# A scan and a mixture of adapters on one core: stores of four chunks in 8 KB rows, x stepped over four chunks, and new orders kept as lists

## The chip, the cores and the metric

The kernel runs on one core of one Trainium2 chip. The metric is the device time of one execution in microseconds (us): median 202.64 of three runs of the kernel before (202.54 to 202.82).

## The reference

Two steps, one after the other. The first is a linear recurrence over time for 8 sequences of 6400 steps and 128 channels; the second treats its 51,200 results as tokens x, finds 8 logits for each, keeps the two largest, and adds to each token the output of the two adapters chosen (rank 16), weighted by a softmax of the two logits.

```python
h = np.zeros((B, D))
for t in range(S):
    h = a[:, t] * h + b[:, t]
    out[:, t] = h
x = out.reshape(B * S, D)
logits = x @ w_gate
topk = np.argpartition(-logits, K, axis=1)[:, :K]          # K = 2
...
for e in range(E):
    ...
    z = x[mask] @ A[e]
    delta[mask] += w[mask, k, None] * (z @ B[e])
return x + delta
```

a and b are 26.2 MB each, the result is 26.2 MB, all float32.

## The kernel before, in words

The tokens are cut into 100 chunks of 512 rows (`C`), four blocks of 128 (`J`). Everything about a chunk carries its number. These are the steps, with the names that the order uses.

- **Loads** `la`, `lb` (L707): a and b, two chunks at a time (512 KB), into one of 6 places (`NL`). A partition holds eight consecutive rows, 4 KB. The first four chunks come singly, in rows of 2 KB.
- **Transposes** `A`, `B`, `P` (L728): PE turns a and b into PSUM (`pA`, `pB`), so that channels are partitions and time runs along the row. `P` does b of one chunk and a of the next together, in 64 x 64 pieces.
- **`ae`** (L746): ACT copies a out of PSUM.
- **Scan** `sc` (L784): DVE's tensor_tensor_scan over 512 steps; its result, in f16, is x transposed, in one of `NX = 24` places `xT`. Scan c needs scan c-1.
- **`Z`, `ze`** (L804, L810): units of six blocks (four at both ends). A block of x is the weight, the router and the eight A matrices side by side are streamed (136 columns); ACT copies the result to `zl`, with room for `NZ = 120` blocks.
- **Gating** (L841 to L880), in groups of up to 24 blocks: `g1` to `g8`, `w1`. Maximum, difference, mask, second maximum, and so on; steps 2, 3, 5, 6 and 7 are on DVE or on POOL (`q`), `w1` is ACT's sigmoid.
- **`mu`** (L913 POOL, L917 DVE): z times the weights. **`T`** (L926): PE turns the product. **`te`** (L932 ACT, L935 DVE): copies it out of PSUM. **`D`** (L940, L941): for each block two matmuls into one bank, x itself (x as the weight, times the identity) and the adapters' output. **`oe`** (L955 ACT, L952 DVE): copies the sum to `outt`, with room for `NO = 72` blocks.
- **Stores** `st` (L986): two chunks at a time, four singles at the end.

A block of x takes every fourth column of a chunk, since a partition of the output holds four consecutive rows (`xblock`, in the function `bass_associative_scan_2x2__then__mixture_of_adapters_kernel`):

```python
def xblock(b):
    return xcols(b // J).rearrange("d (p j) -> d j p", j=J)[:, b % J, :]
...
dst = out[r0 : r0 + m * C, :].rearrange("(h p j) d -> p h j d", p=128, j=J)
view = outt[:, q : q + m * J, :].rearrange("p (h j) d -> p h j d", j=J)
```

So a store of two chunks writes 256 rows of 2 KB. Each engine works through its own list of operations and waits in it for what the next one needs: an operation that has to wait holds all behind it on its engine. SP's list holds loads and stores together. The lists come out of `Program.schedule`: each operation has a rank (a base that grows with its chunk, plus an entry of the table `NUDGE`), and the operations of an engine go out by rank. Which engine does an operation is set by lists of numbers: `TE_ACT` (40 of the 100 `te` go to ACT), `OE_DVE` (7 `oe` to DVE), `MU_DVE` (12 `mu` to DVE), `GATE_DVE` (20 gating steps to DVE). `SPLIT` cuts the store that begins with chunk 68 into 124 and 4 partitions. The ranks give, for the end of SP's list:

```
... la96 st60 lb96 la98 st62 lb98 st64 st66 st68 st70 st72 st74 st76 st78 st80 st82 st84 st86 st90 st88 st92 st94 st98 st97 st99 st96
```

and for PE around the 48th chunk and after the last front transposes:

```
... P47 T31 D30 Z31 D31 T32 P48 D32 Z32 T33 P49 D33 T34 P50 Z33 D34 ...
... B99 T85 T84 Z66 D85 D84 Z67 T87 Z68 T86 D87 T91 D86 T89 T90 D91 T88 D89 D90 D88 T95 T92 T94 T93 D95 D92 D93 D94 T97 T98 D97 D98 T99 T96 D99 D96
```

Of the kernel before, what the change touches and what calls it, by code (L numbers as in the profile page):

```python
# [10 lines left out]
PERIOD = 6  # L11
FREE = {"pe": 0.0, "act": 0.105, "dve": 0.082, "pool": 0.044, "sp": 0.0}
SEEN = {"pe": 0.06, "act": 0.04, "dve": 0.055, "pool": 0.08, "sp": 0.0}
SELF = {"pe": 0.0, "act": 0.035, "dve": 0.035, "pool": 0.078, "sp": 0.0}
PE_WAIT = 0.08
PE_FREE = 0.1
SP_MARGIN = 2.0
LAND_MARGIN = 1.0
Q_RATE = {3: 4.2e-3, 5: 2.1e-3, 7: 2.1e-3}
SCAN_SELF = 0.13  # L20
ISSUE = {"sp": 0.52, "act": 0.45}
LOAD_RATE = 387e3
STORE_RATE = 413e3
DMA_START = 0.3
DMA_SEEN = 1.15
DMA_DEPTH = 9
FIRST_ISSUE = 0.7
FIRST_WORK = 0.73
TABLES = 1.32
NUDGE = {  # L30
# [182 lines left out]
}  # L213
WINDOW = {'pe': 0.0, 'act': 0.0, 'dve': 0.0, 'pool': 0.0, 'sp': 0.0}
START = (-999, "", 0)
FIRST = -9999
EARLY = -400
LEAD = [1, 2]
# [4 lines left out]
FLAT = []  # L223
FILL = {}
# [70 lines left out]
class Program:  # L295
# [5 lines left out]
    def __init__(self):  # L301
        self.ops = []
# [802 lines left out]
```

## Time and profile before

| | |
|---|---|
| median of three runs | 202.64 us |
| profiled execution, first to last instruction | 200.9 us |
| bytes read, written | 52.56 MB, 26.21 MB |
| first scan starts | 6.18 us |
| last load issued by SP | 162.58 us |
| DVE, ACT, PE, POOL busy | 176.2, 175.8, 177.7, 136.9 us |

The profile shows one execution. A group of instructions is named by line, engine, operation and tiles, as out<-in (partitions x elements, type); behind it stand its count, its busy time, the mean of one in ns, and the idle time of the engine just before them with what ended it. PEld is the loading of a matmul's weights, which runs beside PE. SPq is SP's queue of DMA instructions. PE's busy time counts the whole passage of a matmul through the array, so a busy PE isn't PE at its peak.

### The profile page before, as it was taken

The page shows a single profiled execution, that of the slowest core. Times are in us where ns is not written, and L with a number is a line of the kernel's source. Part 1 is how long each engine was busy: PE and PEld are TensorE (multiplying, and loading weights), DVE is VectorE, ACT ScalarE, POOL GpSimd, SP SyncE. Part 2 cuts the span into 40 slices and gives each one's busy share as a digit, 9 for nine tenths or more (in the row PEclk, how much of TensorE's full clock was granted, in tenths as well). Part 3 has the DMA queues.
Part 4 walks back from the last instruction along what each step waited for, and adds up shares of the span by engine and source line. Part 5 has one row for each costly group of instructions (what it writes and reads, how often), then busy time and mean ns, then how long its engine had stood idle before and what let it go on. Part 6 is the DMA issues. An engine that isn't in the chain of part 4 may idle for free.

```text
span 200.9 us, 7611 instructions
## 1 busy us (share of the span) xinstructions
PE 177.7 (88%) x3192; PEld 155.9 (78%) x3192; DVE 176.2 (88%) x283; ACT 175.8 (88%) x327; POOL 136.9 (68%) x176
## 2 busy tenths in 40 slices
PE   6888978999899969999988999899999997898970
PEld 6766867888688858888878888787888886787860
DVE  1699999999999968999897999798899998999971
ACT  2589998999779969999997999899999998899970
POOL 1331559498989887797987797868876466767420
PEclk9999999999999999999999999999999999999998
DMA  6999999999999999999999999999999999999985
GB/s 216 378 412 408 411 405 401 411 406 404 414 409 400 412 416 409 401 417 407 409 413 409 410 409 412 413 410 411 417 408 410 414 410 409 406 381 387 357 338 215
DMA packets 29065, 79.26 MB, mean 395 GB/s; under 512 B 2664, under 2 KB 2920, under 8 KB 29032
## 3 DMA queue, kind: packets, MB, share of 16 engines
q1 hardware_dynamic: 28456, 78.39, 99.0%
q8 instruction: 25, 0.41, 0.8%
q10 hardware_dynamic: 576, 0.40, 0.7%
q14 instruction: 8, 0.07, 0.1%
HBM read 52.56 MB, written 26.21 MB: 392 GB/s over the span
## 4 chain that ended last, share of the span: by engine, by line
DMA 33%; PE 27%; DVE 16%; ACT 15%; SPq 5%; issue 2%; DVEq 0%; ACTq 0%
DMA a_tm<-in_a_dram 26%; DVE xT L784 9%; DMA out_dram<-outt 7%; ACT zl L810 5%; PE pZ L804 5%; SPq L707 5%; PE pB L728 5%; PE pA L728 5%; ACT outt L955 4%; PE pO L940 4%; PE pO L926 4%; ACT a_st L746 4%; PE pO L941 3%; DVE zwT L935 2%; ACT zwT L932 2%
## 5 line engine op out<-in xcount | busy, mean ns | idle before, releaser
L784 DVE TENSOR_TENSOR_SCAN xT<-a_st,xT,pB 128x512 f16<-128x512 f32 x96 | 120.4, 1254 | 7.1 <-PE pA L728 4.3
L913 POOL TENSOR_TENSOR zw<-zl,g 128x512 f16<-128x512 f32 x88 | 92.7, 1067 | 27.9 <-DVE g L880 19.6
L728 PE MATMUL pB<-ident_f,b_tm 64*128 64x64 f32 (+1 forms) x784 | 69.3, 229 | 6.8 <-DMA a_tm<-in_a_dram 6.7
L728 PE MATMUL pA<-ident_f,a_tm 64*128 64x64 f32 (+1 forms) x784 | 69.8, 230 | 0.5 <-DMA b_tm<-in_b_dram 0.3
L746 ACT COPY a_st<-pA 128x512 f32<-128x512 f32 x100 | 63.3, 638 | 4.1 <-PE pA L728 3.3
L728 PEld LDWEIGHTS pB<-ident_f,b_tm 64*128 64x128 f32 (+1 forms) x784 | 56.4, 139 | 11.8 <-DMA a_tm<-in_a_dram 8.3
L810 ACT COPY zl<-pZ 128x816 f32<-128x816 f32 (+1 forms) x69 | 59.7, 865 | 2.0 <-PE pZ L804 1.7
L728 PEld LDWEIGHTS pA<-ident_f,a_tm 64*128 64x128 f32 (+1 forms) x784 | 56.8, 139 | 5.6 <-issue 0.4
L955 ACT COPY outt<-pO 128x512 f32<-128x512 f32 x88 | 55.9, 640 | 3.9 <-PE pO L941 3.0
L940 PE MATMUL pO<-ident_h,xT 128*128 128x128 f16 x368 | 51.6, 222 | 1.3 <-ACT zwT L932 1.0
L941 PE MATMUL pO<-cst_h,zwT 128*128 128x128 f16 x368 | 50.5, 219 | 0.0
L940 PEld LDWEIGHTS pO<-ident_h,xT 128*128 128x128 f16 x368 | 40.2, 113 | 4.3 <-ACT zwT L932 1.4
L804 PE MATMUL pZ<-cst_h,xT 128*128 128x136 f16 x400 | 35.9, 225 | 4.9 <-DVE xT L784 2.0
L941 PEld LDWEIGHTS pO<-cst_h,zwT 128*128 128x128 f16 x368 | 36.8, 100 | 0.0
L926 PE MATMUL pO<-ident_h,zw 128*128 128x128 f16 x368 | 35.2, 220 | 1.4 <-ACT outt L955 1.1
L804 PEld LDWEIGHTS pZ<-cst_h,xT 128*128 128x128 f16 x400 | 26.3, 114 | 9.1 <-DVE xT L784 4.3
L926 PEld LDWEIGHTS pO<-ident_h,zw 128*128 128x128 f16 x368 | 22.9, 97 | 4.7 <-ACT outt L955 1.3
L935 DVE COPY zwT<-pO 128x512 f16<-128x512 f16 x57 | 22.9, 407 | 4.0 <-PE pO L926 3.7
L932 ACT COPY zwT<-pO 128x512 f16<-128x512 f16 x35 | 21.9, 630 | 4.7 <-PE pO L926 4.3
L850 POOL TENSOR_TENSOR L<-k,m 128x192 f32<-128x192 f32 (+2 forms) x16 | 8.4, 524 | 6.2 <-DVE m L848 6.1
L872 POOL TENSOR_TENSOR k<-k,L 128x192 f32<-128x192 f32 (+1 forms) x17 | 9.4, 556 | 4.3 <-DVE L L868 3.0
L846 POOL TENSOR_TENSOR L<-L,k 128x192 f32<-128x192 f32 (+1 forms) x15 | 8.6, 576 | 5.4 <-DVE L L843 4.7
(58 smaller groups left out, 112.2 us busy)
## 6 DMA issues: line engine op xcount, KB each, us to landing
a_tm<-in_a_dram SPq DMA_DIRECT2D x48, 512.0 KB, 13.3
b_tm<-in_b_dram SPq DMA_DIRECT2D x48, 512.0 KB, 13.5
out_dram<-outt SPq DMA_DIRECT2D x47, 512.0 KB, 13.4
a_tm<-in_a_dram SPq DMA_DIRECT2D x4, 256.0 KB, 4.3
out_dram<-outt SPq DMA_DIRECT2D x4, 256.0 KB, 3.6
b_tm<-in_b_dram SPq DMA_DIRECT2D x3, 256.0 KB, 5.1
out_dram<-outt SPq DMA_DIRECT2D x1, 496.0 KB
b_tm<-in_b_dram ACTq DMA_DIRECT2D x1, 256.0 KB, 3.4
```

The costliest lines, as they stand in the source:

```text
L728: last = eng["pe"].transpose(*args)
L746: lambda: eng["act"].copy(a_st[c % NA][:, :], pA[:, c % 2, :]), fr(c, "ae"))
L784: last = eng["dve"].tensor_tensor_scan(out=x[:, s0:s1], data0=a_st[c % NA][:, s0:s1], data1=pB[:, c % 2, s0:s1], initial=init, op0=ALU.mul ...
L804: last = eng["pe"].matmul(pZ[:, k // (n // 2), o : o + W], xblock(b0 + k), Awg_h)
L810: return eng["act"].copy(zl[:, zb : zb + n, :].rearrange("p (h k) w -> p h (k w)", h=2), pZ[:, :, 0 : n // 2 * W])
L913: lambda: eng["pool"].tensor_tensor(out=wv, in0=zv, in1=gv, op=ALU.mult), ba(gi, c, "mu"))
L926: last = eng["pe"].transpose(ptile[:, k * 128 : k * 128 + 128], zz[:, k, :], ident_h[:, :])
L932: lambda: eng["act"].copy(zt, ptile[:, 0 : n * 128]), ba(gi, c, "ta"))
L935: lambda: eng["dve"].tensor_copy(zt, ptile[:, 0 : n * 128]), ba(gi, c, "te"))
L940: eng["pe"].matmul(dst, xblock(b0 + k), ident_h[:, :], start=True, stop=False)
L941: last = eng["pe"].matmul(dst, zt[:, k * 128 : k * 128 + 128], B_h, start=False, stop=True)
L955: lambda: eng["act"].copy(ov, bv), ba(gi, c, "oe"))
```

## The change

1. `STORES`: two stores of two chunks, 23 of four, four singles. In a tile of m chunks a partition holds 4m consecutive output rows, so a store of four has rows of 8 KB. A block of x then takes every 16th column of four chunks, and a z unit needs the scan of the last chunk of its tile. Scans wait, for a place of x, for all `D` of the tile that had it.
2. `NX` 24 to 32, `NO` 72 to 80, `NZ` 120 to 96. Stores take 16 semaphores in turn.
3. The scheduler, its ranks and its costs go; `ORDER` has the list of each engine as text, and an operation runs on the engine in whose list it stands. Counted in them: `te` on ACT 30; `oe` on DVE 2; `mu` on DVE 8; gating steps 2, 3, 5, 6 and 7 on DVE 28.
4. At the start two of the four warm-up transposes between `A0` and `B0` go, and each of the two left becomes 16 transposes of 32 x 32. `sg` (the sigmoid table) is moved ahead of two small loads on ACT, and `zb` ahead of `ms` on POOL.

```diff
-TAIL_UNITS = [4, 4, 4, 4]
-HEAD_UNITS = [4, 4, 4]
-WARM = 16
-NX = 24
-NZ = 120
-NO = 72
-STORE_TAIL = [1, 1, 1, 1]
+UNITS = [4] * 3 + [6] * 62 + [4] * 4
+GROUPS = [1, 2] + [4] * 15 + [2, 1, 1, 1, 1]
+STORES = [2, 2] + [4] * 23 + [1] * 4
+WARM = 14
+NX = 32
+NZ = 96
+NO = 80
+NS = 16
 SPLIT = {68: [124, 4]}
...
+ORDER = {
+    "pe": (
...
+        "T25 P47 T26 Z28 P48 D26 D25 Z29 T28 P49 T27 Z30 P50 D28 D27 P51 T30 Z31 T29 D30 P52 D29 T32 Z32 P53 T31 D32 "
...
+        "D86 D87 T90 Z67 T88 T91 T89 D90 D88 T92 D89 D91 T94 T93 Z68 T95 D92 D93 D94 D95 T97 T96 T98 D96 D98 T99 D97 "
...
+    "sp": (
+        "la0 la1 la2 lb1 lb2 la3 lb3 la4 lb4 la6 lb6 la8 lb8 la10 lb10 la12 lb12 la14 lb14 la16 lb16 la18 lb18 lb20 "
+        "la20 la22 lb22 st0 la24 la26 lb24 st2 lb26 la30 la28 lb28 lb30 lb34 la32 lb32 lb36 la34 la36 la40 lb38 la38 "
+        "lb40 st4 la44 la42 lb42 lb44 st8 la46 lb46 la48 lb48 lb52 la52 la50 lb50 st16 st12 la54 lb56 lb54 la56 lb58 "
+        "la58 la60 la62 lb60 lb62 la64 st20 lb66 st24 lb64 la66 la68 la70 lb70 lb68 st28 st32 la72 la74 lb72 st36 "
+        "lb74 la76 lb78 lb76 la78 st40 la80 lb80 la82 lb84 lb82 la84 st44 la86 la88 lb86 lb88 st48 la90 lb90 la92 "
+        "st52 lb92 la94 lb94 la96 st56 lb96 la98 st60 lb98 st72 st64 st68 st80 st76 st84 st88 st92 st96 st98 st97 "
+        "st99 "
...
         def xblock(b):
-            return xcols(b // J).rearrange("d (p j) -> d j p", j=J)[:, b % J, :]
+            s0, n = tile_of[b // J]
+            o = s0 % NX * C
+            return xT[:, o : o + n * C].rearrange("d (p j) -> d j p", p=128)[:, b - s0 * J, :]
...
-            c1 = (b0 + n - 1) // J
+            c1 = sum(tile_of[(b0 + n - 1) // J]) - 1
...
-            xlast[ch % NX] = o_D[c]
+            s0, m = tile_of[c]
+            for k in range(s0, s0 + m):
+                if xlast.get(k % NX, (None, []))[0] != s0:
+                    xlast[k % NX] = (s0, [])
+                xlast[k % NX][1].append(o_D[c])
...
-            dst = out[r0 : r0 + m * C, :].rearrange("(h p j) d -> p h j d", p=128, j=J)
-            view = outt[:, q : q + m * J, :].rearrange("p (h j) d -> p h j d", j=J)
+            dst = out[c * C : (c + m) * C, :].rearrange("(p j) d -> p j d", p=128)
+            view = outt[:, q : q + m * J, :]
...
+        def warm_up(k):
+            def f(e):
+                if k < WARM0:
+                    return e.transpose(pO[:, 0, 0:128], ident_f[:, :], ident_f[:, :])
+                for j in range(4):
+                    for r in range(0, 128, 32):
+                        rows, bank = ident_f[r : r + 32, :], (pO if r < 64 else pZ)[:, r // 32 % 2, :]
+                        last = e.transpose(bank[:, 32 * j : 32 * j + 32], rows, rows[:, r : r + 32])
+                return last
+            return f
```

More of the change, by code (lines that the diff above doesn't have):

```diff
@@ L285 @@
 }
 class Op:
-    __slots__ = (
-        "i", "eng", "name", "dur", "deps", "emit", "base", "kind", "k", "sem", "locks", "cnt", "clock", "parts",
-    )
+    __slots__ = ("i", "eng", "name", "n", "deps", "emit", "sem", "cnt", "clock", "parts", "may")
 class Program:
@@ L302, in __init__, with add @@
         self.ops = []
-    def add(self, eng, name, dur, deps, emit, at, sem=None, locks=False, parts=1):
+        self.where = {name: e for e in ORDER for name in ORDER[e].split()}
+    def add(self, may, name, n, deps, emit, sem=None, parts=1):
         op = Op()
         op.i = len(self.ops)
-        op.eng, op.name, op.dur, op.emit = eng, name, dur, emit
-        op.base, op.kind, op.k = at
-        op.deps = [d for d in deps if d is not None]
-        op.sem, op.locks = sem, locks or eng == "pool"
-        op.cnt, op.clock, op.parts = 0, None, parts
+        op.may = may.split()
+        op.eng = self.where.get(name, op.may[0])
+        assert op.eng in op.may
+        op.name, op.n, op.emit = name, n, emit
+        op.deps = deps
+        op.sem, op.cnt, op.clock, op.parts = sem, 0, None, parts
@@ L398, in schedule, with waits @@
                     op.cnt = n
-    def waits(self, sems, dma_sems):
+    def waits(self):
         dma_cnt = {}
@@ L411, in waits @@
                     op = self.order[e][at[e]]
-                    if any(d.clock is None for d, _ in op.deps):
+                    if any(d.clock is None for d in op.deps):
                         break
@@ L475, in bass_associative_scan_2x2__then__mixture_of_adapters_kernel @@
     NU = len(units)
-    GMAX = 4
-    stores = []
-    c0 = 0
-    for n in [2] * ((NCH - sum(STORE_TAIL)) // 2) + STORE_TAIL:
+    stores, tile_of, c0 = [], {}, 0
+    for n in STORES:
         stores.append((c0, n))
+        assert c0 % NX + n <= NX and c0 * J % NO + n * J <= NO
+        for c in range(c0, c0 + n):
+            tile_of[c] = (c0, n)
         c0 += n
     assert c0 == NCH
-    groups = []
-    u0 = 0
-    for n in LEAD + [GMAX] * ((NU - sum(LEAD) - sum(TAPER)) // GMAX) + TAPER:
+    groups, u0 = [], 0
+    for n in GROUPS:
         groups.append((u0, n))
@@ L490, in bass_associative_scan_2x2__then__mixture_of_adapters_kernel @@
     assert u0 == NU
-    bbase = []
-    for u0, n in groups:
-        e = (units[u0 + n - 1][0] + units[u0 + n - 1][1]) // J - PERIOD
-        bbase.append(max(e, bbase[-1] + PERIOD * last / GMAX) if bbase else e)
-        last = n
-    gfirst = [units[u0][0] // J for u0, n in groups]
     glast = [(units[u0 + n - 1][0] + units[u0 + n - 1][1]) // J - 1 for u0, n in groups]
@@ L552, in bass_associative_scan_2x2__then__mixture_of_adapters_kernel @@
         outt = sbuf("outt", [128, NO, 128], F32)
-        GB = GMAX * U
+        GB = max(sum(m for _, m in units[u0 : u0 + n]) for u0, n in groups)
         m1 = sbuf("m1_", [128, GB], F32, 2)
@@ L748, in front @@
-        def front(c):
-            r0 = rows[c]
-            o_fi = []
-            for k in range(FILL.get(c, 0)):
-                o_fi.append((P.add(
-                    "pe", f"fi{c}_{k}", 0.109, [(o_id, True)] + get(o_sc, c - 2),
-                    lambda: eng["pe"].transpose(pB[:, c % 2, 0:128], ident_f[:, :], ident_f[:, :]), fr(c, "fi")), True))
+            o_ae[c] = P.add("act", f"ae{c}", J, [o_A[c]] + get(o_sc, c - NA),
+                            lambda e: e.copy(a_st[c % NA][:, :], pA[:, c % 2, :]))
@@ L755, in front, with load_next @@
+        def load_next(c):
+            if c < NCH and c not in o_la:
+                load(c, 1 if c < HEAD else HC)
+        def front(c):
+            load_next(c)
             if not woven(c):
-                o_A[c] = P.add("pe", f"A{c}", 0.109 * J, deps_a(c), trans(part_a(c)), fr(c, "A"))
-                o_B[c] = P.add("pe", f"B{c}", 0.109 * J, deps_b(c) + o_fi, trans(part_b(c)), fr(c, "B"))
+                o_A[c] = P.add("pe", f"A{c}", J, deps_a(c), trans(part_a(c)))
+                o_B[c] = P.add("pe", f"B{c}", J, deps_b(c), trans(part_b(c)))
@@ L853, in maxes @@
-            def maxes():
-                for k in range(nb):
-                    last = eng["dve"].max(out=t8[:, k, :], in_=Lp[:, k, :])
-                return last
-            def first():
-                return eng["dve"].tensor_reduce(out=v1, in_=Lp, axis=X, op=ALU.max)
-            d1 = P.add("dve", f"g1_{gi}", 0.09 + 0.075 * nb if top else 0.142 + nb * E * 1.04e-3,
-                       [(o_ze[u], True) for u in range(u0, u0 + n)] + old, maxes if top else first, ga(gi, "g1"))
+                return P.add("dve" if kind == 8 else "pool dve", f"g{kind}_{gi}", nb, deps, f)
@@ L863, in gating @@
+            top = nb <= TOP8
+            ready = [o_ze[u] for u in range(u0, u0 + n)] + old
             if top:
+                t8 = v8[s][:, 0:nb, :]
                 b1, b2 = (t8[:, :, k : k + 1].to_broadcast([128, nb, E]) for k in (0, 1))
-                d2 = wide(2, [(d1, True)] + old,
-                          lambda e: e.tensor_tensor(out=kk, in0=Lp, in1=b1, op=ALU.subtract))
-                d5 = wide(6, [(d1, True)] + old,
-                          lambda e: e.tensor_tensor(out=ll, in0=Lp, in1=b2, op=ALU.subtract))
-            else:
-                d2, d5 = search()
@@ L871, in gating, with maxes @@
-            d6 = wide(7, [(d2, True), (d5, True)],
-                      lambda e: e.tensor_tensor(out=kk, in0=kk, in1=ll, op=ALU.add))
-            a1 = P.add("act", f"w1_{gi}", 0.19 + nb * E * 0.86e-3, [(d6, True)] + old,
-                       lambda: eng["act"].activation(sg, kk, ACTF.Sigmoid), ga(gi, "w1"))
+                def maxes(e):
+                    for k in range(nb):
+                        last = e.max(out=t8[:, k, :], in_=Lp[:, k, :])
+                    return last
+                d1 = P.add("dve", f"gx_{gi}", nb, ready, maxes)
@@ L875, in gating @@
+            d6 = wide(7, [d2, d5], lambda e: e.tensor_tensor(out=kk, in0=kk, in1=ll, op=ALU.add))
+            a1 = P.add("act", f"w1_{gi}", nb, [d6] + old, lambda e: e.activation(sg, kk, ACTF.Sigmoid))
             for u in range(u0, u0 + n):
@@ L899, in back_part @@
-        def back_part(gi, ch, c, b0, n):
             u0 = groups[gi][0]
+            b0 = c * J
             q0 = b0 - units[u0][0]
             w = c % NW
-            us = [u for u in range(u0, u0 + groups[gi][1]) if units[u][0] < b0 + n and units[u][0] + units[u][1] > b0]
-            gv = g[gi % NG][:, q0 : q0 + n, :].unsqueeze(3).broadcast_to([128, n, E, R])
+            us = [u for u in range(u0, u0 + groups[gi][1]) if units[u][0] < b0 + J and sum(units[u]) > b0]
+            gv = g[gi % NG][:, q0 : q0 + J, :].unsqueeze(3).broadcast_to([128, J, E, R])
@@ L918, in back_part @@
-            for k in range(n):
+            zv = zl[:, zp : zp + J, 0:128].rearrange("p q (e r) -> p q e r", e=E)
+            zz, zt = zw[w], zwT[w][:, :]
+            wv = zz[:, :, :].rearrange("p q (e r) -> p q e r", e=E)
+            o_mu[c] = P.add("pool dve", f"mu{c}", J, [o_ze[u] for u in us] + [o_g[gi]] + get(o_T, c - NW),
+                            lambda e: e.tensor_tensor(out=wv, in0=zv, in1=gv, op=ALU.mult))
+            for k in range(J):
                 zlast[zp + k] = o_mu[c]
@@ L937, in delta, with tr @@
-            def delta():
-                for k in range(n):
+            def tr(e):
+                for k in range(J):
+                    last = e.transpose(ptile[:, k * 128 : k * 128 + 128], zz[:, k, :], ident_h[:, :])
+                return last
+            o_T[c] = P.add("pe", f"T{c}", J, [o_mu[c], o_ih] + free + (o_wu if c < 2 else []), tr)
+            o_te[c] = P.add("dve act", f"te{c}", J, [o_T[c]] + get(o_D, c - NW),
+                            lambda e: copy(e, zt, ptile[:, 0:C]))
@@ L939, in delta @@
+            def delta(e):
+                for k in range(J):
                     dst = bank[:, k * 128 : k * 128 + 128]
-                    eng["pe"].matmul(dst, xblock(b0 + k), ident_h[:, :], start=True, stop=False)
-                    last = eng["pe"].matmul(dst, zt[:, k * 128 : k * 128 + 128], B_h, start=False, stop=True)
-                return last
-            o_D[c] = P.add("pe", f"D{c}", 0.11 + 0.112 * n, [(o_te[c], True)], delta, ba(gi, c, "D"))
-            xlast[ch % NX] = o_D[c]
@@ L956, in back_part @@
-            for k in range(n):
+                    e.matmul(dst, xblock(b0 + k), ident_h[:, :], start=True, stop=False)
+                    last = e.matmul(dst, zt[:, k * 128 : k * 128 + 128], B_h, start=False, stop=True)
+                return last
+            o_D[c] = P.add("pe", f"D{c}", J, [o_te[c]], delta)
+            s0, m = tile_of[c]
[3 more added lines that the diff above has]
+                xlast[k % NX][1].append(o_D[c])
@@ L957, in back_part @@
+            o0 = b0 % NO
+            ov = outt[:, o0 : o0 + J, :].rearrange("p k w -> p (k w)")
+            o_oe[c] = P.add("act dve", f"oe{c}", J,
+                            [o_D[c]] + distinct(olast[o0 + k] for k in range(J) if o0 + k in olast),
+                            lambda e: copy(e, ov, bank[:, :]))
+            for k in range(J):
                 olast[o0 + k] = o_oe[c]
@@ L1012, in load_next, with fronts @@
-        def load_next(c):
-            if c not in o_la:
-                load(c, 1 if c < HEAD else HC)
-        nf, nb = 0, 0
+        def fronts(c):
+            s0, n = tile_of[c]
+            return s0 + n
+        nf, nb, ns = 0, 0, 0
         for gi, (u0, n) in enumerate(groups):
@@ L1032, in bass_associative_scan_2x2__then__mixture_of_adapters_kernel @@
                 nb += 1
+                if sum(stores[ns]) == nb:
+                    store(*stores[ns])
+                    ns += 1
         P.schedule()
-        waits = P.waits(s_eng, s_dma)
+        waits = P.waits()
         def run(name, handle):
@@ L1045, in run @@
                 else:
-                    for part in inst if op.parts > 1 else [inst]:
+                    for part in inst if isinstance(inst, list) else [inst]:
                         part.then_inc(s_dma[op.sem], 16)
```

496 lines of the change are left out of this document (116 added, 380 removed), and 232 rows, old and new, of tables (NUDGE, ORDER).

## The prediction, made before the result was known

> **What bounds the kernel now.** I read the page's slices first, then busy time and DMA rate by stage, then the chain that ended last, and last the groups of instructions.
>
> ```profile
> span 200.9 us, 7611 instructions
> PE 177.7 (88%) x3192; PEld 155.9 (78%) x3192; DVE 176.2 (88%) x283; ACT 175.8 (88%) x327; POOL 136.9 (68%) x176
> q1 hardware_dynamic: 28456, 78.39, 99.0%
> HBM read 52.56 MB, written 26.21 MB: 392 GB/s over the span
> ```
>
> Three engines stand at 88%, and the one queue that carries all loads and stores at 99% of the sixteen DMA engines' time. The stages say where each of them decides; the columns are the stretch, its length, busy time of PE, PEld, DVE, ACT and POOL (number of instructions), granted clock, DMA share, GB/s.
>
> ```profile
> 10.00:175.00 165.00, 151.18 (x2841) 132.18 (x2839) 153.19 (x217) 152.83 (x281) 123.31 (x150) 1.00 1.03 410
> 12.00:34.00 22.00, 18.50 (x359) 15.44 (x356) 20.99 (x28) 19.64 (x35) 11.15 (x16) 1.00 1.03 408
> 175.00:180.00 5.00, 5.00 (x91) 4.51 (x91) 4.57 (x8) 4.88 (x10) 3.03 (x6) 1.00 1.01 381
> 178.00:185.00 7.00, 6.36 (x103) 5.52 (x100) 7.00 (x25) 6.92 (x16) 4.26 (x6) 1.00 1.03 393
> 185.00:196.00 11.00, 9.46 (x148) 8.16 (x146) 8.96 (x30) 9.05 (x20) 3.90 (x10) 1.00 0.92 348
> ```
>
> From 10 to 175 the DMA engines are never free (1.03; records overlap a little) and move 410 GB/s, while DVE and ACT are idle 165 - 153.2 = 11.8 and 165 - 152.8 = 12.2 us. After 185 it turns: DMA falls to 0.92 and 348 GB/s, because stores wait for results. So the time up to the end of the loads is set by bytes and by time per row; the end, by DMA and engines together.
>
> ```profile
> DMA 33%; PE 27%; DVE 16%; ACT 15%; SPq 5%; issue 2%; DVEq 0%; ACTq 0%
> 8.19 13.38 DMA a_tm<-in_a_dram
> 61.88 12.06 DMA a_tm<-in_a_dram
> 93.53 12.40 DMA a_tm<-in_a_dram
> 113.09 14.03 DMA a_tm<-in_a_dram
> 158.23 13.43 DMA out_dram<-outt
> 171.70 0.32 issue
> ```
>
> The chain that ended last (start, length, what) tells the other half. It goes through five transfers, together 65.3 us; between 127 and 158 and from 171.7 to the end it holds compute alone. Both limits lie close together, so a cheaper transfer is not passed on whole.
>
> **The change part by part. Rows of the stores (gain 4.9 us of DMA time).** 92 of 100 chunks go out as 23 stores of four chunks, 128 rows of 8 KB in place of 512 rows of 2 KB; on each of 16 engines 23 x 8 = 184 rows of 8 KB for 736 of 2 KB. No 8 KB row of this queue is in the trace, so I extend the two lengths that are. From 12 to 34 only loads run, in 4 KB rows: 16 x 4096 B / 408 GB/s = 160.6 ns a row. From 178 to 185 only stores run: 16 x 2048 / 393 = 83.4 ns. So 2 KB more cost 77.2 ns, a row has 6.2 ns that do not depend on its length, and 8 KB cost 160.6 + 154.4 = 315.0. Four short rows cost 333.6: gain 18.6 ns, times 184 = 3.4 us. By the stretch 175 to 180 (381 GB/s, the last loads ending in it) the short row costs 86.0, the fixed part is 11.4, the long row 309.8, the gain 34.2 ns x 184 = 6.3 us. I take the middle, 4.9 us; ends 3.4 and 6.3. Below that stands only the case that a long store row gains nothing, kept as a rival.
>
> The Trainium skill (DMA: Bandwidth & Descriptors, section "Why small descriptors are slow") gives each packet about 3 cycles on top of one cycle per 32 B. By it four 2 KB rows take 4 x 67 = 268 cycles and one 8 KB row 259, an estimate of 3.4% of the stores' time, some 2.1 us in place of 4.9; the rows above show more per row than that.
>
> Where it counts: in the new SP list, as in the old, the stores of 64 chunks stand ahead of the last load. So 64/100 x 4.9 = 3.1 us are passed on as loads that land earlier, and 1.8 us fall into the end, where DMA is at 0.92 and waits for results; I pass on half, 0.9. Sum: 4.0 us. For this the engines must do their work from 10 to 175 in 3.1 us less, leaving DVE 8.7 idle of 11.8.
>
> **Work moved between engines (none on the path).**
>
> ```profile
> L935 DVE COPY zwT<-pO 128x512 f16<-128x512 f16 x57 | 22.9, 407 | 4.0 <-PE pO L926 3.7
> L932 ACT COPY zwT<-pO 128x512 f16<-128x512 f16 x35 | 21.9, 630 | 4.7 <-PE pO L926 4.3
> L955 ACT COPY outt<-pO 128x512 f32<-128x512 f32 x88 | 55.9, 640 | 3.9 <-PE pO L941 3.0
> L952 DVE COPY outt<-pO 128x512 f32<-128x512 f32 x4 | 2.7, 674 | 0.1
> L917 DVE TENSOR_TENSOR zw<-zl,g 128x512 f16<-128x512 f32 x12 | 8.3, 695 | 0.0
> L913 POOL TENSOR_TENSOR zw<-zl,g 128x512 f16<-128x512 f32 x88 | 92.7, 1067 | 27.9 <-DVE g L880 19.6
> ```
>
> Counted in the lists: copies `te` on ACT 40 to 30, on DVE 60 to 70; copies `oe` on ACT 93 to 98, on DVE 7 to 2; products `mu` on DVE 12 to 8, on POOL 88 to 92; gating steps 2, 3, 5, 6, 7 on DVE 20 to 28. ACT: -10 x 0.630 + 5 x 0.640 = -3.1 us. DVE: +10 x 0.407 - 5 x 0.674 - 4 x 0.695 = -2.1, plus eight gating steps of 0.2 to 0.35, so about zero. POOL: +4 x 1.067 less eight steps, about zero, with 27.9 us idle ahead of its products. DVE stays at 176 us and has to fit into some 4 us less. Nothing of ACT's 3.1 is added: it is what lets it keep pace.
>
> **Waiting for whole tiles (taken as nothing).** A z unit now needs all scans of its four-chunk tile, up to three scans more, and each store four `oe` in place of two. Behind such a z stand, on PE, the next transposes and `T`, `D`, and behind those the scans. The lists allow for it: at P48 the old one has 32 z units and 32 `D` behind it, the new one 29 and 25. The places that pay for the longer lag are the added ones (x 24 to 32 chunks, output 18 to 20); z falls from 120 to 96 blocks, four groups, with products about 15 chunks behind z in the new lists and 24 chunks of room. If that cover fails, a scan stands late in DVE's queue: the engine-bound rival.
>
> **SP's queue (nothing).** 24 issues fewer. A store of four at its head holds the loads behind it; what covers it is what is already queued:
>
> ```profile
> out_dram<-outt SPq DMA_DIRECT2D x47, 512.0 KB, 13.4
> SPq L986 <- ACT outt L955: 16.2, 11, 2.7
> 162.58 1.77 SPq L707 DMA_DIRECT2D b_tm<-in_b_dram  x1
> 164.39 33.59 SPq L986 DMA_DIRECT2D out_dram<-outt  x21
> ```
>
> 13.4 us from issue to landing, against a longest wait of SP for an `oe` of 2.7 us; and after the last load only stores are left. The cut of store 68 into 124 and 4 partitions stays, on a store twice as long; no row shows how the parts spread, and I take nothing.
>
> **The start (nothing).** Between A0 and B0 four 128-wide transposes give way to 32 small ones.
>
> ```profile
> 5.00 0.63 PE L611 MATMUL pO<-ident_f 128*128 128x128 f32 x4
> 5.46 0.60 PE L728 MATMUL pB<-ident_f,b_tm 128*128 128x128 f32 x4
> 6.18 1.22 DVE L784 TENSOR_TENSOR_SCAN xT<-a_st,pB 128x512 f16<-128x512 f32 x1 [3.98 <-PE pB L728]
> 19.06 0.27 PE L728 MATMUL pB<-ident_f,b_tm 64*128 64x64 f32 x1 [0.22 <-DMA a_tm<-in_a_dram]
> ```
>
> The four start 0.46 us before B0. Thirty-two cost between that and 32 x 0.115 = 3.7 us; I take 1 us more. It delays the first scan but not the loads, and at 19 us PE waits for a load, so it has caught up by then. Without that cover: 1 us.
>
> **x read in longer steps (taken as nothing).** x is the weight of 400 z and 400 `D` matmuls; its step goes from 4 elements (8 B) to 16 (32 B).
>
> ```profile
> L804 PEld LDWEIGHTS pZ<-cst_h,xT 128*128 128x128 f16 x400 | 26.3, 114 | 9.1 <-DVE xT L784 4.3
> L940 PEld LDWEIGHTS pO<-ident_h,xT 128*128 128x128 f16 x368 | 40.2, 113 | 4.3 <-ACT zwT L932 1.4
> L941 PEld LDWEIGHTS pO<-cst_h,zwT 128*128 128x128 f16 x368 | 36.8, 100 | 0.0
> 129.77 0.27 PE L728 MATMUL pA<-ident_f,a_tm 64*128 64x64 f32 x1
> 134.80 0.27 PE L728 MATMUL pB<-ident_f,b_tm 64*128 64x64 f32 x1
> ```
>
> Four times the step (2 B to 8 B) costs 113 - 100 = 13 ns of a load; the same again makes 126. Loads lie beside the matmul before them, except the first of a group: 169 groups x 13 ns = 2.2 us of PE. PE's own pace is (134.80 - 129.77) / 3 = 1.68 us a chunk in a stretch without idle time, against 0.786 MB / 410 GB/s = 1.92 for DMA: 0.24 us a chunk cover 0.02.
>
> **Sum.** 200.9 - 4.0 = 196.9 us for the profiled execution. The median stands 202.64 - 200.9 = 1.7 us above it: 202.64 - 4.0 = **198.6 us**; with the ends of the row's price and all or half of the end passed on, 196.4 to 200.2.
>
> **The rivals.** (A) The engines become the bound. For it: over half the chain is compute, and DVE's total does not fall. Against it: 12 us of idle time in the middle. Then only the chain's transfers shrink, by 4.9 of some 193 us of DMA work, 2.5%: 65.3 x 0.025 = 1.6 us, 201.0; range 200.2 to 202.2.
>
> (B) 8 KB rows gain nothing: stores at the rate they have. For it: nothing of this queue shows such a row; against it: 4 KB beat 2 KB. 202.6.
>
> (C) Slower: the loads of x no longer hide behind matmuls. Place: PE, eight loads of x a chunk. It decides from 0.24 / 8 = 30 ns a load beyond the 56 ns that a matmul covers. If a load occupies PE for its whole present 113 ns, 57 ns x 8 = 0.46 us a chunk: 2.14 against 1.92, over some 93 chunks +20 us, 223. Against it: the step of 8 B left the pace alone. The Trainium skill (SBUF — State Buffer, section "Door 1: The DMA port swizzle", the note on cachelines) holds that two reads of each 16-byte line are needed for full rate; 8 B steps give two, 32 B steps one, so by that rule this case would come. The trace disagrees in part: 8 B steps already cost 13 ns.
>
> (D) Slower: a store of four at SP's head waits so long that the queued 13.4 us run out. The fourth `oe` comes three chunks, 5.8 us, after the first; a hold of 20 us leaves DMA dry for 6.6, less 4.0: 205.2. It decides from 13.4 + 4.0 = 17.4 us. Against it: the longest hold now is 2.7.
>
> **How the numbers follow.** Forecast 0.53, A 0.25, B 0.07, C 0.06, D 0.09. A measurement can tell about 0.2% (0.4 us) from no change. Faster: 0.53 + 0.25 = 0.78; within: 0.07; slower: 0.15. The range goes from the forecast's lower end over A and B, to 203.0: 196.4 to 203.0.
>
> **What would show it.** Right: the rate from 10 us on near 416 GB/s, the store-only stretch above 400, the last load issued near 159.5, the last scan near 178. The rows: far fewer packets, some 8 KB ones. Wrong: DMA share below 1 between 40 and 165 (A or D: in D with SP waiting for `oe`; in A with DVE or ACT at 97%); a flat 410 (B); `PEld` of xT far over 126 ns and PE over 1.9 us a chunk (C); the first scan after 8 us with no wait for loads near 20 (the start).

## The result: slower by 3%

The changed kernel takes 208.29 us in the median of four runs (208.05 to 210.18) where the kernel before takes 202.63 (202.54 to 202.82): ratio 1.0302 [1.0279, 1.0325]. The prediction, 198.6 us and 78% for faster, was wrong. The profiled execution of the changed kernel is its longest (210.18 us, span 208.2); the other three have spans of 206.1 to 206.5.

First the page of the changed kernel: span, busy times, the main queue, the bytes, packets, the granted clock in 40 slices, and the chain's shares.

```profile
span 208.2 us, 7646 instructions
PE 187.6 (90%) x3220; PEld 166.0 (80%) x3220; DVE 175.0 (84%) x292; ACT 176.4 (85%) x322; POOL 136.8 (66%) x172
PEclk9995599999999999999999999999999999999995
DMA packets 19609, 79.26 MB, mean 381 GB/s; under 512 B 2296, under 2 KB 2552, under 8 KB 16632
q1 hardware_dynamic: 19000, 78.39, 94.2%
HBM read 52.56 MB, written 26.21 MB: 378 GB/s over the span
PE 45%; DMA 37%; ACT 6%; SPq 4%; DVE 3%; issue 1%; ACTq 0%
```

The change did what it says: q1 has 19000 packets for 28456, with the same bytes. DVE and ACT do as much as before, PE 10 us more. But the queue that was never free is busy 94.2% of the span for 99.0%. Transfers became cheaper, and the DMA engines stand idle instead. The stretches say where (columns as in the prediction); first the changed kernel:

```profile
10.00:175.00 165.00, 157.59 (x2803) 139.76 (x2804) 150.18 (x216) 151.38 (x273) 120.53 (x149) 0.97 1.00 402
30.00:40.00 10.00, 9.61 (x174) 8.17 (x170) 9.56 (x13) 9.87 (x20) 6.78 (x8) 1.00 0.74 276
40.00:160.00 120.00, 117.34 (x2140) 105.12 (x2140) 111.17 (x161) 114.84 (x207) 96.56 (x118) 1.00 1.02 410
40.00:46.00 6.00, 5.55 (x105) 4.86 (x106) 5.28 (x8) 5.86 (x11) 3.26 (x6) 1.00 1.01 363
46.00:160.00 114.00, 111.79 (x2039) 100.27 (x2037) 105.88 (x154) 108.98 (x197) 93.31 (x112) 1.00 1.02 413
175.00:180.00 5.00, 4.96 (x91) 4.55 (x90) 4.83 (x9) 4.41 (x7) 4.31 (x6) 1.00 0.97 398
178.00:185.00 7.00, 6.46 (x98) 5.48 (x97) 6.83 (x22) 5.77 (x12) 4.17 (x7) 1.00 0.70 287
185.00:196.00 11.00, 7.77 (x121) 7.08 (x119) 7.90 (x29) 7.90 (x19) 4.69 (x4) 1.00 0.81 299
190.00:195.00 5.00, 2.21 (x34) 1.84 (x31) 2.28 (x9) 2.06 (x5) 1.52 (x2) 1.00 0.71 277
```

and four stretches of the kernel before that the prediction does not show:

```profile
30.00:40.00 10.00, 9.30 (x176) 8.00 (x175) 9.49 (x13) 9.07 (x17) 7.31 (x9) 1.00 1.03 406
40.00:160.00 120.00, 112.31 (x2116) 99.03 (x2118) 110.25 (x156) 112.51 (x210) 97.77 (x116) 1.00 1.03 410
46.00:160.00 114.00, 106.53 (x2006) 94.01 (x2006) 104.46 (x149) 106.83 (x200) 92.11 (x110) 1.00 1.03 410
190.00:195.00 5.00, 3.69 (x60) 3.18 (x58) 4.41 (x11) 3.91 (x9) 1.36 (x3) 1.00 0.91 340
```

There are two holes. From 30 to 40 the DMA engines move 276 GB/s for 406. From 190 to 195 they move 277 for 340, and PE, DVE, ACT and POOL are idle more than half of the time. In between, where the gain was to come, the stretch from 40 to 160 shows the rate of before, 410, but only because the end of the first hole lies in it (363 up to 46). From 46 on the rate is 413 for 410: the long rows do bring something.

**The first hole.** SP's waits for `oe` in the changed kernel between 20 and 45 us (total, times, longest); its issues there; the same store's issue in the kernel before:

```profile
SPq L624 <- ACT outt L298: 11.4, 2, 9.7
```

```profile
25.76 0.33 SPq L401 DMA_DIRECT2D b_tm<-in_b_dram  x1
35.80 0.35 SPq L624 DMA_DIRECT2D out_dram<-outt  x1
```

```profile
24.97 0.40 SPq L986 DMA_DIRECT2D out_dram<-outt  x1
```

After `lb22` (25.76) SP stands at `st0` for 10 us, and the next load, `la24`, goes out behind it. On twelve of the sixteen engines `lb22` has landed by 34.5 us; from there they have nothing until 36.6. `st0` waits for `oe1`, and that for `D1`. In PE's old list `D1` stands behind `P12`, in the new one behind `P17`, five chunks later, while `st0` stands one load earlier.

**The second hole.** The chain around the cut store 68 (start, length, what), then ACT's copy behind it with its wait in brackets:

```profile
172.27 0.54 SPq L624
172.86 20.01 DMA out_dram<-outt
```

```profile
192.94 0.59 ACT L298 COPY outt<-pA 128x512 f32<-128x512 f32 x1 [3.02 <-DMA out_dram<-outt]
```

The part with 124 partitions (992 KB) is issued at 172.27, the one with 4 at 172.86, and the store has landed at 192.9. ACT's next `oe` needs its places and waits 3.02 us, with PE and DVE behind it. Of the sixteen landings of store 80, issued after it, twelve come by 189.1 and four at 191.7 to 195.3: four engines carry that part alone. The Trainium skill says so beforehand (DMA: Bandwidth & Descriptors, "Why a DMA increments its semaphore by 16 and not by 1"): such a transfer uses the largest number of engines up to 16 that divides its outer dimension, for 124 that is 4. The trace agrees.

Two things more differ. The granted clock is 0.5 from 15.4 to 25.6 us, in the profiled execution. And the weight loads of x take 144 to 147 ns for 113 to 114:

```profile
L493 PEld LDWEIGHTS pZ<-cst_h,xT 128*128 128x128 f16 x400 | 31.1, 147 | 4.2 <-DVE xT L475 1.3
L581 PEld LDWEIGHTS pO<-ident_h,xT 128*128 128x128 f16 x368 | 46.2, 144 | 3.3 <-ACT zwT L298 0.7
L582 PEld LDWEIGHTS pO<-cst_h,zwT 128*128 128x128 f16 x368 | 39.5, 108 | 0.3 <-issue 0.3
```

### The profile page after: what moved, and what is told of

Read it like the earlier page. It is cut to its first block, busy times and chain, and to the rows that moved or that the text cites. A ratio compares the mean times of both kernels' runs of the same rounds, so it can differ in the third digit from the quotient of the medians.

```text
span 208.2 us, 7646 instructions
## 1 busy us (share of the span) xinstructions
PE 187.6 (90%) x3220; PEld 166.0 (80%) x3220; DVE 175.0 (84%) x292; ACT 176.4 (85%) x322; POOL 136.8 (66%) x172
## 3 DMA queue, kind: packets, MB, share of 16 engines
q1 hardware_dynamic: 19000, 78.39, 94.2%
## 4 chain that ended last, share of the span: by engine, by line
PE 45%; DMA 37%; ACT 6%; SPq 4%; DVE 3%; issue 1%; ACTq 0%
DMA out_dram<-outt 19%; PE pB L422 16%; DMA b_tm<-in_b_dram 13%; PE pZ L493 9%; PE pO L581 7%; PE pO L571 6%; PE pO L582 5%; DMA a_tm<-in_a_dram 4%; SPq L401 3%; ACT outt L298 2%; ACT zl L499 2%; ACT a_st L440 1%; PE pA L422 1%; DVE xT L475 1%; ACT zwT L298 1%
## 5 line engine op out<-in xcount | busy, mean ns | idle before, releaser
L562 POOL TENSOR_TENSOR zw<-zl,g 128x512 f16<-128x512 f32 x92 | 96.6, 1069 | 32.1 <-DVE g L547 25.3
L422 PE MATMUL pB<-ident_f,b_tm 64*128 64x64 f32 (+1 forms) x784 | 72.7, 235 | 5.0 <-DMA b_tm<-in_b_dram 2.6
L422 PE MATMUL pA<-ident_f,a_tm 64*128 64x64 f32 (+1 forms) x784 | 73.0, 236 | 0.0
L440 ACT COPY a_st<-pA 128x512 f32<-128x512 f32 x100 | 59.3, 606 | 10.6 <-PE pA L422 10.2
L581 PEld LDWEIGHTS pO<-ident_h,xT 128*128 128x128 f16 x368 | 46.2, 144 | 3.3 <-ACT zwT L298 0.7
L493 PEld LDWEIGHTS pZ<-cst_h,xT 128*128 128x128 f16 x400 | 31.1, 147 | 4.2 <-DVE xT L475 1.3
L298 DVE COPY zwT<-pO 128x512 f16<-128x512 f16 x64 | 26.3, 415 | 5.4 <-PE pO L571 4.8
L298 ACT COPY zwT<-pO 128x512 f16<-128x512 f16 x28 | 16.6, 601 | 0.5 <-PE pO L571 0.3
L535 POOL TENSOR_TENSOR k<-zl,m 128x192 f32<-128x192 f32 (+1 forms) x15 | 7.7, 510 | 9.6 <-DVE m L534 9.6
L475 DVE TENSOR_TENSOR_SCAN xT<-a_st,pB 128x512 f16<-128x512 f32 (+1 forms) x8 | 7.5, 940 | 4.9 <-PE pB L422 4.7
```

Source lines behind the costliest of these rows:

```text
L298: return e.copy(dst, src) if e is eng["act"] else e.tensor_copy(dst, src)
L422: last = e.transpose(*args)
L440: lambda e: e.copy(a_st[c % NA][:, :], pA[:, c % 2, :]))
L475: last = e.tensor_tensor_scan(out=x[:, s0:s1], data0=a_st[c % NA][:, s0:s1], data1=pB[:, c % 2, s0:s1], initial=init, op0=ALU.mult, op1=AL ...
L493: last = e.matmul(pZ[:, k // (n // 2), o : o + W], xblock(b0 + k), Awg_h)
L535: d2 = wide(2, [d1] + old, lambda e: e.tensor_tensor(out=kk, in0=Lp, in1=bc(v1), op=ALU.subtract))
```

## The experiments

The theory: long rows are a gain, lost to three stalls (SP behind `st0`, the clock at the start, the cut store 68). The rival: x in steps of 32 B makes PE the bound, and the stalls only show that. Ratios are to the kernel before.

**1. Each suspect alone, on the changed kernel.**

```diff
e1_rows2k    xblock per chunk (step 4), rows of 2 KB: dst "(h p j) d -> p h j d", j=J
e2_nosplit   -SPLIT = {68: [124, 4]}   +SPLIT = {}
e3_oldwarm   -A0 wu12 wu13 B0   +A0 wu12 wu13 wu14 wu15 B0   (each one 128-wide transpose)
e4_st0       -lb22 st0 la24 la26 lb24 st2 lb26 la30 la28 lb28 lb30
             +lb22 la24 la26 lb24 lb26 la30 la28 lb28 st0 lb30 st2
```

> The changed kernel with its lists, places and stores of four chunks, but each store in 512 rows of 2 KB and x read in steps of four elements (8 B), as before the change. If the long rows are a gain and the loss lies in the stalls at the start and the end, this kernel loses the gain and keeps the stalls: 208.3 + 2.4 (what the loads made up between 42 and 179 us) + some of the end = 210.5 to 212, with a rate near 410 GB/s in the middle. Rival: reading x in 32 B steps (144 to 147 ns a weight load in place of 113) makes PE the bound and costs more than the rows bring: then it is faster than the changed kernel, 205 to 207.5. If the two cancel: 208.0 to 208.8.

> The changed kernel with store 68 sent as one transfer of 128 rows in place of 124 and 4. Theory: the part of 124 rows went on four DMA engines only, landed 20 us after its issue, and ACT's copies into the places that it held waited 3.0 us for it; whole, it lands within 13 us and nobody waits: 208.3 - 3 to 4 = 204.3 to 205.3, with DMA over 370 GB/s from 190 to 195. Rival: the end is set by the results, which are late anyway, and the wait only moves to another one: 207.6 to 208.5.

> The changed kernel with the warm-up of before: four 128-wide transposes between A0 and B0 in place of 32 small ones. Theory: the small ones leave PE short of work in its first microseconds, and with the waits at 11 to 16 us the granted clock falls to 0.5 from 15.4 to 25.6 us; with the old ones it stays at 1.0 and the loads of chunk 24 land up to 4.6 us earlier, of which the rest of the kernel keeps 1.5 to 4: 204.3 to 206.8. Rival: the clock fell because PE waited 1.8 us at 16 for a late load, whatever the warm-up: the same dip and 207.8 to 208.8. Second rival: the dip goes, but SP's hold behind store 0 alone makes DMA run dry: full clock and still 207.5 to 208.3.

> The changed kernel with stores 0 and 2 placed later in SP's list: behind the loads of chunk 28 and behind lb30, the loads in their old order. Theory: SP no longer holds the loads of chunk 24 for 10 us behind store 0, DMA does not run dry at 35 to 39 us, and 1 to 3 us come back: 205.3 to 207.3. Rival: PE, at half clock until 25.6 us and busy 99% afterwards, is what sets the loads' pace; loads queued earlier only wait in the queue: 207.8 to 208.6, with the same DMA gap a few us later.

- `e1_rows2k`: ratio 1.040 [1.036, 1.044], 2 us slower than the changed kernel by the ratios, 3 by the medians. Not the rival: undoing rows and step together loses time. Without the stalls the same edit costs 1.2 us (`e11` against `e6_all`, below); why it costs more beside them is not settled.
- `e2_nosplit`: 204.55 us, 1.0070 [1.0041, 1.0098]: 3.7 us back, as expected, and the hole from 190 to 195 closes:

```profile
190.00:195.00 5.00, 4.31 (x69) 3.86 (x68) 4.88 (x27) 4.92 (x13) 2.14 (x3) 1.00 0.85 346
```

- `e3_oldwarm`: 208.73, 1.0286 [1.0255, 1.0318]: nothing. The clock stayed at 1.0 from 10 to 40 in this profile, and the time did not move: the rate from 30 to 40 is better, 349 GB/s, but the hole from 190 to 195 is deeper, 159.
- `e4_st0`: 206.97, 1.0198 [1.0176, 1.0220]: 1.3 back. DMA runs on from 30 to 40, but the hole at the end takes back a part (224 GB/s from 190 to 195):

```profile
30.00:40.00 10.00, 9.75 (x180) 8.51 (x182) 9.50 (x13) 9.86 (x19) 7.50 (x10) 1.00 1.03 407
190.00:195.00 5.00, 3.62 (x43) 3.51 (x44) 2.80 (x18) 4.31 (x11) 1.07 (x1) 0.78 0.53 224
```

**2. Together, the start, the step, and a control.** `e6_all` has the edits of `e2`, `e3` and `e4`, and `st64 st68 st72 st76 st80` for `st72 st64 st68 st80 st76`. `e9_nosplit_oldwarm` has those of `e2` and `e3`. `e5_x8b` is `e2` with `xblock` per chunk and the stores unchanged. `e8_before_nosplit` is the kernel before with `SPLIT = {}`.

> Four edits on the changed kernel together: store 68 in one piece, the old warm-up, stores 0 and 2 behind the loads of chunk 28 and lb30, and store 72 behind 64 and 68. Theory: the stalls are where the loss is and the long rows are a gain; without them the forecast's gain shows: 204.6 (store 68 in one piece alone) - 1.3 (store 0 alone) - 1 to 2 (no dip of the clock; within the runs of the former kernel those with a clock of 0.99 take 203.2, those with 0.973 205.0) = 200.5 to 202.5, below the 202.7 of before. Rival: PE, 99% busy from 40 to 160 us, is the bound and gives nothing back for an earlier start: 202.8 to 204.5.

> Store 68 in one piece and the old warm-up. With the stall at the end gone, the start can be seen. Theory of the warm-up: the granted clock no longer falls at the start in any run, and all runs lie with the quicker ones of the kernel with the small transposes: 202.8 to 203.8 against 204.55. Rival: the dip comes from waits for late loads, by chance, whatever the warm-up: the same mixture, median 204.2 to 205.

> Store 68 in one piece, and x read in steps of four elements (8 B) while the stores keep their 8 KB rows; each token's result therefore goes to another token's place in the output, all counts of work are unchanged. It shows the price of the longer steps by itself, against 204.55 for store 68 in one piece. Theory: weight loads go from 144 to 147 back to 113 to 115 ns, PE's busy time in the middle falls by 3 to 5%, and as PE is 99% busy there, 1 to 2.5 us come back: 202.0 to 203.5. Rival: the loads are hidden beside the matmuls and DMA sets the pace: 204.2 to 204.9.

> A control on the kernel before: store 68 in one piece. Its part of 124 rows landed at 189.3 us and ACT waited 0.66 us there. Theory: the cut did harm only because the store had become twice as long and the places were claimed sooner: here 202.0 to 202.9, no difference beyond 0.3%. Rival: it was a loss there too: 200.5 to 201.9.

- `e6_all`: 201.95, 0.9959 [0.9945, 0.9974], quicker than both kernels. The stalls were the loss.
- `e9`: 204.57, 1.0081 [1.0052, 1.0109], the same as `e2`, with the same scatter (203.22 to 205.12). Its profile has the dip too, from 19.9 to 23.3 us, so the old warm-up does not prevent it. What starts the dip of the clock stays open.
- `e5`: 203.95, 1.0060 [1.0034, 1.0087] against `e2`'s 1.0070: the intervals overlap, so this decides nothing on the step.
- `e8`: 203.54, 1.0040 [1.0029, 1.0051]. Neither theory: in the kernel before the cut is worth 0.9 us. The same cut is a gain there and costs 3.7 here; why it helps there is not settled. The trace of the kernel before also speaks against what the expectation says of it: the part of 124 rows landed at 181.0 us there, and ACT's wait of 0.66 us, at 172, was for an earlier store.

**3. What the rows and the step are worth without stalls.** On `e6_all`: `e10_x8b` (8 KB rows, step 8 B), `e11_rows2k` (2 KB rows, 8 B), `e12_rows4k` (4 KB rows, 16 B). `e13_dma_only` has transfers alone.

> The kernel with all four edits (201.95 us), and x read in steps of 8 B while the stores keep rows of 8 KB, so each token's result goes to another token's place in the output; all counts of work are unchanged. Theory: what the rows gain is held back by PE, which is busy 19.2 to 20.0 us of every 20 from 40 to 160 us; with weight loads of x back at 113 ns DMA sets the pace again and the time falls to 200.0 to 201.2. Rival: DMA already sets the pace and the longer step is free: 201.6 to 202.2.

> The kernel with all four edits, and stores in rows of 2 KB with x in steps of 8 B: rows and step undone together, everything else kept. Theory: the rows gain more than the step costs, so this is slower than 201.95: 203.0 to 205.0, with a rate of 408 to 410 GB/s in the middle. Rival: the rows' gain does not come through and the step costs: 200.8 to 202.0.

> The kernel with all four edits, rows of 4 KB and x in steps of 16 B: half way. If the gain per row falls with its length and the weight load at 16 B costs no more than at 8 B, this has most of the gain and none of the loss: 200.8 to 201.9 with weight loads of x at 113 to 120 ns. Rival: loads at 130 ns or more and about half of the rows' gain: 202.0 to 203.0.

> No computation: only transfers from SP, in five phases that each end before the next begins: loads (4 KB rows) and stores in a ratio of 2 to 1 as in the kernel, with the stores in 2 KB rows; the same with 8 KB rows; stores alone in 2 KB rows; stores alone in 8 KB rows; loads and stores with 4 KB rows. It prices the row by itself. The prediction's price: 333.6 ns for four 2 KB rows against 315.0 (ends: 344.0 against 309.8), so stores alone at 393 (381) GB/s in 2 KB rows and 416 (423) in 8 KB rows, and 404 to 408 against 412 to 416 mixed. Rival: long store rows gain less than 1%, and the rate that the changed kernel gained in its middle has another cause.

- `e10`: 201.75, 0.9959 [0.9947, 0.9971]: the ratio of `e6_all`. The longer step costs nothing that can be told, as the rival had it.
- `e11`: 203.12, 1.0026 [1.0017, 1.0036]. So the rows alone (`e11` to `e10`) bring 203.12 - 201.75 = 1.4 us, not 4.0.
- `e12`: 202.25, 0.9977 [0.9966, 0.9989], in between, with weight loads of x at 144 to 146 ns, as its rival had them.

The middle of `e11`, of `e10` and of `e6_all`, in this order:

```profile
40.00:160.00 120.00, 115.77 (x2158) 101.47 (x2156) 110.63 (x162) 113.92 (x210) 97.24 (x117) 1.00 1.03 409
```

```profile
40.00:160.00 120.00, 115.97 (x2163) 101.77 (x2161) 110.95 (x163) 114.44 (x210) 97.06 (x118) 1.00 1.02 413
```

```profile
40.00:160.00 120.00, 118.25 (x2162) 106.15 (x2161) 111.32 (x163) 115.24 (x210) 97.34 (x117) 1.00 1.02 413
```

The rows raise the rate from 409 to 413 GB/s, 1%, though the DMA engines' busy time per byte falls by 2% (share 1.03 at 409, 1.02 at 413). The step costs PE 118.25 - 115.97 = 2.3 us of busy time in 120, and the rate stays. `e13`, a single execution, by stretches: loads with stores of 2 KB rows, with 8 KB rows, stores alone of 2 KB, stores alone of 8 KB (columns: stretch, length, POOL, clock, DMA share, GB/s):

```profile
14.00:22.00 8.00, 0.00 (x0) 1.00 1.03 413
...
56.00:64.00 8.00, 0.00 (x0) 1.00 1.03 421
...
94.00:99.00 5.00, 0.00 (x0) 1.00 1.04 381
...
108.00:112.00 4.00, 0.00 (x0) 1.00 1.02 424
```

Stores alone gain 11% (381 to 424). Mixed with loads, the stream as a whole gains 2% (413 to 421; 406 to 420, over 3%, where 28 us of each phase are taken). Stores are a third of the bytes there, so 11% of their time would be some 3.5% of the whole, an estimate: most of it comes through. The prediction's price gives 2% for this mixture, so `e13` bears the price out; the kernel, with 1%, gets less than the transfers alone.

**4. Are the engines the reason that only 1.4 us arrive, and what of the end?** `e14_light8` and `e15_light2` are `e6_all` and `e11` with work left out (expectation). `e16_split64` is the changed kernel with `{68: [64, 64]}`; `e17_nosplit_st0` has the edits of `e2` and `e4` only.

> The kernel with all four edits, 8 KB rows and x in 32 B steps, with work left out: the matmul with B that adds the adapters' part is dropped (four of the eight matmuls of each output, so the output is only x) and the copy before it takes 128 of 512 columns. PE, ACT and DVE lose some 20, 14 and 21 us. Theory (the engines hold the rows' gain back): the rate from 40 to 160 rises from 413 to 417 to 420 GB/s, and this kernel is 3 to 5 us quicker than the same with 2 KB rows. Rival (transfers beside compute gain only 1%): 413 to 414, and 1 to 1.6 us between the two.

> The same work left out (no matmul with B, 128 of 512 columns copied), with stores in rows of 2 KB and x in steps of 8 B. Theory: DMA sets the pace here already, 408 to 410 GB/s from 40 to 160, so taking work away moves the middle little: 200.5 to 203. Rival: the engines held this one back as well, and its rate rises above 412.

> The changed kernel with store 68 cut into 64 and 64 partitions in place of 124 and 4. Theory: the cut itself is harmless; the harm is that 124 partitions of 8 KB, 992 KB, go on four DMA engines: as quick as the uncut one, 203.5 to 205.3. Rival: any cut of that store costs, 207.5 to 209.

> The changed kernel with store 68 in one piece and stores 0 and 2 placed later, with its own warm-up and with store 72 still ahead of 64 and 68. Theory: the two gains add, as one lies at the start and one at the end: 204.55 - 1.3 = 203.2, and store 72's place accounts for the other 1.3 of 201.95. Rival: the four edits' gain is these two alone, more than their sum because the start's gain showed only in part behind the stall at the end: 201.7 to 202.3.

Middle of `e14`, then of `e15`:

```profile
40.00:160.00 120.00, 109.02 (x1909) 95.03 (x1907) 103.21 (x162) 109.80 (x210) 97.87 (x118) 0.97 1.02 413
```

```profile
40.00:160.00 120.00, 107.26 (x1896) 90.74 (x1894) 102.61 (x163) 108.71 (x210) 97.43 (x117) 0.96 1.03 410
```

- `e14` 201.16 (0.9920 [0.9906, 0.9934]), `e15` 202.57 (0.9991 [0.9980, 1.0001]): 1.4 us between them, as with all the work, and the same 413 and 410 GB/s, though PE and ACT now have 10 us free. The engines do not hold the rows' gain back, and the theory of `e14` falls. The gain is that small in this stream, and what keeps it smaller than in `e13` stays open.
- `e16`: 204.33, 1.0076 [1.0050, 1.0101], as quick as uncut. Not the cut, but its 124 partitions on four engines.
- `e17`: 201.86, 0.9954 [0.9940, 0.9968]. Two edits give all of `e6_all`; store 72's place and the warm-up give nothing. From 30 to 40 and from 190 to 195 it has

```profile
30.00:40.00 10.00, 9.50 (x178) 8.19 (x175) 9.49 (x14) 9.86 (x20) 6.85 (x9) 1.00 1.03 410
190.00:195.00 5.00, 3.99 (x57) 3.07 (x54) 3.03 (x12) 3.98 (x10) 1.83 (x2) 1.00 0.97 399
```

## Why the prediction was wrong, by its own steps

The medians put the change together. Each step is one run against another, so its error is some 0.3 us, and some 0.6 where `e2` stands in it, whose runs lie between 202.85 and 205.42:

| step | from, to | us |
|---|---|---|
| lists, places, whole tiles, with the four edits, old rows and step | before 202.59, `e11` 203.12 | +0.5 |
| rows 2 KB to 8 KB | `e11`, `e10` 201.75 | -1.4 |
| x in steps of 32 B | `e10`, `e6_all` 201.95 | +0.2 |
| old warm-up and store 72's place given up | `e6_all`, `e17` 201.86 | -0.1 |
| stores 0 and 2 early in SP's list | `e17`, `e2` 204.55 | +2.7 |
| store 68 cut 124 and 4 | `e2`, changed kernel 208.29 | +3.7 |
| sum | | +5.6 (measured 5.66) |

The last two steps depend on their order: with stores 0 and 2 moved first, their place counts 1.3 us (`e4` against the changed kernel) and the cut 5.1 (`e17` against `e4`). By the ratios in place of the medians they are 2.4 and 4.7. The cut is the larger one each way, and each of the two alone makes the kernel slower than before (`e2`, `e4`).

- **SP's queue (nothing): failed, and it is the first of two steps that turned the sign.** The prediction set a cover of 13.4 us, a median over the whole kernel, against a longest wait of 2.7, a wait of the old lists. In the new lists the wait is 9.7 us, and what was queued at that moment lasted 34.5 - 25.8 = 8.7. Rival D had the mechanism (DMA share under 1, SP waiting for `oe`), with the wrong point from which it decides (17.4 us), the wrong store (the first of four chunks; it was the first of two) and a chance of 0.09. Its price of 205.2 is near what this stall alone leaves, 204.55, by luck: it set 6.6 us dry less 4.0 for the rows, where the runs show 2.7 (`e17` to `e2`) less 0.7 (before to `e17`). The issues are 23 fewer (53 to 30), not 24. Two lists show the lateness without a run: `D1` behind `P17`, `st0` ahead of `la24`.
- **The cut of store 68 ("I take nothing"): failed, the largest term, 3.7 us.** In the kernel before, the part of 124 partitions was half as large and landed 15 us after its issue (166.2 to 181.0), about as its neighbours did (13 to 14); here it took 20, and uncut in `e2` the store took 15. The prediction saw that it doubles, had no row on how it spreads, and put it at nothing without a bound. A transfer that doubles and whose spread is unknown was reason enough to look for who waits for its places.
- **Rows (gain 4.9 us of DMA time, 4.0 passed on): the price held, passing it on failed.** By the packet records from 46 to 160 us a 2 KB row took 84.9 ns in `e11` and an 8 KB row 312.7 in `e10`: 4 x 84.9 - 312.7 = 27 ns a row, times 184 = 5.0 us, as priced. But 1.4 us arrive. The last load lands at 175.9 us in `e11` and at 174.9 in `e10`, 1.0 earlier where the prediction passed on 3.1; 0.4 more come at the end, where it had 0.9. The step that failed is that DMA time saved in the middle is time gained: the packets' time per byte falls by 2%, but the rate rises by 1%, and their records overlap less (share 1.03 to 1.02). Why is open; the engines' work is not the reason (`e14`, `e15`). The Trainium skill's fixed cost per packet (DMA: Bandwidth & Descriptors, "Why small descriptors are slow") gave the prediction an estimate of 2.1 us. That this is nearer to 1.4 is luck, as it speaks of the packet's own time: it has 3.4%, and the packets here show 8% (339.6 to 312.7).
- **Work moved, whole tiles (nothing): nearly held.** What is left after rows, step and stalls is +0.5 us. It includes the cut that is missing in `e11` and was worth 0.9 in the kernel before, so it leaves no loss for the lists themselves.
- **The start (nothing): right on the warm-up** (`e3`, `e9`). The dip of the clock was not foreseen. In `e2`'s runs low clock and long times go together: 0.986 to 0.991 with 202.9 to 203.6 us, 0.973 to 0.974 with 204.8 to 205.4. In `e9` and `e16` they do not: there 0.984 to 0.987 stand beside 205.1. In the four profiled executions with store 0 early and store 68 not on four engines, the time goes with the rate from 30 to 40 us (346, 328, 310 and 278 GB/s in `e9`, `e5`, `e2` and `e16`: 203.22, 204.06, 204.91 and 205.07 us), not with the dip (3.4, 6.8, 10.2 and 3.4 us long). In `e6_all` and `e17` a dip remains and the times agree within 0.3 us. So what scatters is the first hole; whether the dip has a part in it, no run sets.
- **x in longer steps (nothing): right in effect, the estimate too low.** 144 to 147 ns, not 126; PE's busy share from 40 to 160 rises to 98.5% in `e6_all`, and this still costs nothing that can be told. Of rival C the trigger was true and the price not. The Trainium skill (SBUF — State Buffer, "Door 1: The DMA port swizzle") has two reads of each 16-byte line needed for full rate. The loads of `e10`, `e12` and `e6_all` bear out that an edge lies between 8 and 16 B (below), though 8 B is not free either, and show nothing like the slowdown that rival C took from it.
- **Rivals A and B.** `e14` and `e15` speak against A, the engines as the bound. B, no gain from rows, falls by `e10` and `e11`; the changed kernel's 413 GB/s from 46 us on lie midway between its 410 and the forecast's 416.

## What to carry to other kernels

When the lists are new, the waits of the old trace say nothing: look in the new lists for the last operation that a store at the head of the queue needs, count how many loads' work stands ahead of it, and compare with what is queued at that point, not with a median. A packet's price can be right and the time still not come: here 2% less packet time per byte brought 1% more rate, so look for a stretch that shows how packet time becomes rate before passing it on whole. An old special case (here the cut into 124 and 4) is a new edit as soon as what it applies to doubles, and needs a price of its own.

## What the runs showed of the hardware

The weight load depends on the step of its columns in a stair: 100 to 108 ns at 2 B (zwT), 113 to 115 at 8 B, 144 to 147 at 16 B and at 32 B. The rows are of `e10` (8 B), `e12` (16 B) and `e6_all` (32 B):

```profile
L487 PEld LDWEIGHTS pZ<-cst_h,xT 128*128 128x128 f16 x400 | 26.8, 115 | 5.3 <-DVE xT L469 0.9
```

```profile
L487 PEld LDWEIGHTS pZ<-cst_h,xT 128*128 128x128 f16 x400 | 31.0, 146 | 5.1 <-ACT zl L493 0.9
```

```profile
L485 PEld LDWEIGHTS pZ<-cst_h,xT 128*128 128x128 f16 x400 | 31.0, 147 | 4.1 <-ACT zl L491 0.7
```

Stores alone ran at 381 GB/s in 2 KB rows and at 424 in 8 KB rows; with two bytes loaded for each one stored the stream ran at 413 and 421 (one execution, `e13`). In the changed kernel the landings of the store behind the transfer of 124 partitions came some 6 us later on four DMA engines than on the other twelve.
